# Rounding float64 weights between products: loads issued by SP, a chunk rounded three products after its load, and an earlier first norm

## The chip, the cores and the metric

The kernel runs on one core of a Trainium2 chip. The metric is the device time of one execution in microseconds (us); for the kernel before it is 1148.23 us, the median of three runs (1146.14 to 1149.64). The engines are TensorE (PE, matmuls), VectorE (DVE), ScalarE (ACT), GpSimd (POOL) and SyncE (SP, which here only issues DMA transfers). Each works through its own list of instructions and waits on semaphores for the others.

## The reference, cut to what matters

A retention block (attention with a fixed decay in place of softmax) feeds a gated feed-forward block with an RMS norm. The weights w_gate, w_val and w_out come as float64, so the kernel has to round them to float32 on the chip.

```python
def _attn_ref(q, k, v):                       # q, k, v: (8, 8, 576, 64) float32
    scores = scale * np.matmul(q, k.transpose(0, 1, 3, 2))
    ret = scores * Dmat[None, :, :, :]        # Dmat: gamma[head] ** (row - column), causal
    return np.matmul(ret, v).astype(np.float32)

def _moe_ref(x, w_gate, w_val, w_out, rms_g): # x: (4608, 512); w_gate, w_val: (512, 1536) float64
    rms = np.sqrt(np.mean(x * x, axis=-1, keepdims=True) + 1e-06)
    xn = x / rms * rms_g
    g = xn @ w_gate
    silu = g * (1.0 / (1.0 + np.exp(-g)))
    val = xn @ w_val
    return (silu * val @ w_out).astype(np.float32)   # w_out: (1536, 512) float64
```

## The kernel before

The attention is cut into **jobs**: one pair of heads of one batch entry, or a part of it. `slot(j)` computes the scores and states of job j on PE, weighs them and sums the states on DVE, and finishes job j - 1 (`values`, `carried`), which writes a block of `x`. The tokens are cut into twelve **units** of 384. A unit's norm is a chain over several engines: `square` (ACT), `gather` (DVE, adds the squares), `norm_1` (mean on PE, root on POOL), `diagonals` (DVE), `norm_2` (a broadcast product `rb` on PE, then four scalings of x on DVE).

The first two units run as plain products while the weights are still arriving. The float64 weights come in 18 **chunks** of 1 MB: for each third g of the hidden features two chunks of w_gate and two of w_val (chunks 0 to 11), then six of w_out (12 to 17). There are four spare places for chunks that have landed and are not yet rounded; the last six use only three of them.

```python
    LATER = (1, 2, 3, 2, 3, 3)
    def spare(i):
        return i % 4 if i < n_up else LATER[i - n_up]      # n_up = 12

    def load_chunks(n, queue=nc.scalar):                   # nc.scalar: the issue stands in ACT's list
        while n_loads < min(n, len(chunks)) and waits_at.get(spare(n_loads)) is None:
            load_chunk(n_loads, queue)
            n_loads += 1
```

Rounding a chunk takes five DVE instructions over 128x1024 elements and three ACT instructions. `exponent` is the first that reads the landed chunk. After the third instruction of `mantissa` the place is free and the next load is issued. The generator `rounding` fixes the order; `weights(n)` takes n steps of it and stands behind each product.

```python
    def exponent(i):
        nc.vector.tensor_scalar(out=e, in0=words_of[i][..., 1::2], ...)          # L871
        acts.extend(...)                    # three ACT instructions, L887, given out by act()

    def mantissa(i):
        nc.vector.tensor_scalar(out=dst.bitcast(U32), in0=hi, ...)               # L898
        yield
        nc.vector.scalar_tensor_tensor(out=dst, in0=lo, ...)                     # L903
        yield
        act(chunk=i)                        # what is left of this chunk's ACT instructions
        nc.vector.scalar_tensor_tensor(out=e, in0=hi, in1=e, ...)                # L908
        waits_at[spare(i)] = None

    def join(i):
        nc.vector.scalar_tensor_tensor(out=dst, in0=dst, in1=exp_of.pop(i), ...) # L916

    def rounding():
        for i in range(len(chunks)):
            if i not in exp_of and i in words_of:
                exponent(i)
                yield
            for ahead in (True, False):
                if i + 1 in words_of and i + 1 not in exp_of and i > (1 if ahead else 0):
                    exponent(i + 1)
                    yield
                if ahead:
                    yield from mantissa(i)
                    load_chunks(i + 5 if i else 0)
                    yield
            join(i)
            n_chunks += 1
            yield
```

A plain product is four matmuls of 128x384 into a bank of PSUM; five banks go round for these products, for the jobs' values and for the norms. ACT (silu) or DVE (multiply) empties the bank.

```python
    def up_plain(u, m, g):
        for half in range(2):
            for i in (2 * g, 2 * g + 1):
                ps = bank(f"up_{u}_{m}_{half}_{i}")
                for c in range(NHP):
                    nc.tensor.matmul(ps[:, :U], lhsT=w_up[m][:, 4 * half + c, ...], rhs=x_of[u][:, c], ...)  # L652
                h = h_of[u][:, half * NH + i]
                if m:
                    nc.vector.tensor_tensor(out=h, in0=h, in1=ps[:, :U], op=ALU.mult)   # L658
                else:
                    nc.scalar.activation(out=h, in_=ps[:, :U], func=AF.Silu)            # L660
                yield
```

The first eight jobs and then the 48 products of the two units, with jobs 8 to 11 put behind products 29, 33, 37 and 41 (and the end of job 11 behind 45):

```python
        for j in range(2 * NHP):                           # NHP = 4
            slot(j)
            if j + 1 < 2 * NHP:
                turn(j + 1)                                # transposes on PE, copies on ACT
            if squares:
                gather(*squares.pop())
            for i in ((1,), (2,), (3,), (4, 5), (6,), (7,), (), ())[j]:
                scale_v(i)
            if j:
                u, c = divmod(j - 1, NHP)
                squares.append((u, c, square(u, c)))
            act(1)
            if j == 5:
                norm_1(0)
            elif j == 6:
                norm_2(0)
            weights((2, 0, 0, 1, 1, 1, 1, 0)[j])
            if j == 4:
                gather(*squares.pop())
            elif j == 5:
                diagonals(0)
            act(1)
        ...
        load_qk(2 * NHP)                                   # 13 loads of a job, issued by SP
        load_kv(2 * NHP)
        made = combine_out()                               # four combinations of w_out on DVE, L690
        step = -1
        for m, g in [(m, g) for g in range(NG) for m in range(2)]:
            for u in range(2):
                weights_to(4 * g + 2 * m + 1)
                for i, _ in enumerate(up_plain(u, m, g)):
                    step += 1
                    later(step)                            # jobs 8 to 11; loads of the jobs behind them
                    ...                                    # end of job 7 and norm of unit 1
                    weights(2)
                    act(1)
                    if u and m and g == NG - 1:
                        weights_to(len(chunks))
                        next(made, None)
                    if i == 1:
                        weights_to(4 * g + 2 * m + 2)
        ...
        rest = across(1)                                   # products with w_out, L726; the first is xo,
        next(rest)                                         # the second, zo, reads t1 of differences(), L710
```

From unit 2 on, a Strassen-like scheme with seven products instead of eight is used; it is not touched.

Of the kernel before, what the change touches and what calls it, by code (L numbers as in the profile page):

```python
# [41 lines left out]
def kernel(  # L42
# [11 lines left out]
    nc = tc.nc  # L54
# [3 lines left out]
    NHP = H // 2  # L58
# [421 lines left out]
    def gather(u, c, sq):  # L480

        if c == NHP - 1 and u > 2:
            nc.vector.scalar_tensor_tensor(
                out=t_of[u], in0=t_of[u], scalar=EPS * DM / P, in1=sq, op0=ALU.add, op1=ALU.add
            )
        elif c:
            nc.vector.tensor_tensor(out=t_of[u], in0=t_of[u], in1=sq, op=ALU.add)
        else:
            t_of[u] = sq
# [5 lines left out]
    def norm_1(u):  # L495

        ms = bank(f"ms_{u}")
        for s in range(NS):
            nc.tensor.matmul(
                ms[:, s : s + 1], lhsT=t_of[u][:, s * P : s * P + P], rhs=mean_w,  # L500
                start=True, stop=True,
            )
        r = tmp.tile([P, NS], F32, tag="r", name=f"r_{u}", bufs=1)
        nc.vector.tensor_scalar(out=r, in0=ms[:, :NS], scalar1=EPS, scalar2=None, op0=ALU.add)
        nc.gpsimd.tensor_tensor(out=r, in0=r, in1=mhalf.to_broadcast([P, NS]), op=ALU.pow)
        t_of[u] = r
# [324 lines left out]
    for f in range(0, NF, 2):  # L831
        chunks.append((w_out[:, f : f + 2], moe_w_out, slice(f * P, f * P + 2 * P), slice(None)))
    LATER = (1, 2, 3, 2, 3, 3)
    words_of, exp_of, waits_at = {}, {}, {}
    n_chunks = n_loads = 0

    free = w_up[0][:, 8:].rearrange("p b f -> p (b f)")
# [5 lines left out]
    def load_chunk(i, queue):  # L843
        dst, src, rws, cols = chunks[i]
        if src.dtype != F32:
            n = dst.shape[1]
            cols = slice(2 * (cols.start or 0), 2 * cols.stop if cols.stop else None)
            src = src.bitcast(U32)
            at = spare(i)
            dst = free[:, : 4 * DM] if at == 3 else (  # L850
                w_out[:, 4 * at : 4 * at + 4].rearrange("p c f -> p (c f)")
            )
            dst = words_of[i] = dst.bitcast(U32).rearrange("p (c f) -> p c f", c=n)
            waits_at[at] = i
        queue.dma_start(out=dst, in_=src[rws, cols].rearrange("(c p) f -> p c f", p=P))

    def load_chunks(n, queue=nc.scalar):

        nonlocal n_loads
# [3 lines that stand above are left out]
# [21 lines left out]
    def act(n=0, chunk=-1):  # L884

        while acts and (n > 0 or acts[0][0] <= chunk):
            nc.scalar.activation(func=AF.Relu, **acts.pop(0)[1])  # L887
            n -= 1
# [43 lines left out]
    def rounding():  # L932

        nonlocal n_chunks
        for i in range(len(chunks)):
            if i not in exp_of and i in words_of:
                exponent(i)
                yield
            for ahead in (True, False):
                if i + 1 in words_of and i + 1 not in exp_of and i > (1 if ahead else 0):  # L940
                    exponent(i + 1)
                    yield
                if ahead:
                    yield from mantissa(i)
                    load_chunks(i + 5 if i else 0)
                    yield
            join(i)
            n_chunks += 1
            yield
# [4 lines left out]
    def weights(n):  # L954

        for _ in range(n):
            next(steps, None)

    def weights_to(n):

        while n_chunks < min(n, len(chunks)):
            next(steps)

    def start():

        h_of[0] = ffn.tile([P, NF, U], F32, tag="h", name="h_0")
        tables = list(zip((causal, gv, gc, gq, gx), (_causal_table(), *_decay_tables(H, D))))

        def table(i, queue):
            t, values_ = tables[i]
            src = nc.inline_tensor(values_, name=t.tensor.name + "_table")
            queue.dma_start(out=t, in_=src.ap())

        make_identity(nc, ident)
        nc.scalar.activation(out=tick, in_=mhalf[:1], func=AF.Silu)
        nc.vector.memset(ones, 1.0)
        warm = bank("warm")
        for _ in range(6):  # L980
            nc.tensor.matmul(warm[:, :P], lhsT=ones, rhs=ones, start=True, stop=True)
        first_places.update(find_places())
        load_chunks(1)
        for i in (1, 0, 2):
            table(i, nc.scalar)
        weights(3)
        for j in range(2 * NHP):
            load_first(j, {0: range(2), 1: range(2, H)}.get(j))
            if j == 1:
                table(3, nc.sync)  # L990
            load_chunks((1, 1, 1, 1, 2, 2, 2, 3)[j], nc.sync)
        table(4, nc.sync)
        nc.sync.dma_start(out=rms_g, in_=moe_rms_g.rearrange("(c p) -> p c", p=P))
        load_chunks(4, nc.sync)
        turn(0)
        scale_v(0)
        act(3)
        squares = []

        def later(step):  # L1000

            if step == LATER_AT[0] - 8:
                following(2 * NHP - 1)
            elif step in LATER_AT:
                j = 2 * NHP + LATER_AT.index(step)
                if j < LATER_JOBS:
                    slot(j, rest=(j > 2 * NHP))
                    if j + 1 < LATER_JOBS:
                        following(j)
                else:  # L1010
                    values(j - 1)
                    carried(j - 1)

        for j in range(2 * NHP):
            slot(j)
            if j + 1 < 2 * NHP:
                turn(j + 1)
# [4 lines that stand above are left out]
            if j:  # L1022
                u, c = divmod(j - 1, NHP)
                squares.append((u, c, square(u, c)))
            act(1)
            if j == 5:
                norm_1(0)
            elif j == 6:
                norm_2(0)
            weights((2, 0, 0, 1, 1, 1, 1, 0)[j])  # L1030
            if j == 4:
                gather(*squares.pop())
            elif j == 5:
                diagonals(0)
            act(1)
        gather(*squares.pop())
        load_qk(2 * NHP)
        load_kv(2 * NHP)
        made = combine_out()
        step = -1  # L1040
        for m, g in [(m, g) for g in range(NG) for m in range(2)]:
            for u in range(2):
                weights_to(4 * g + 2 * m + 1)
                for i, _ in enumerate(up_plain(u, m, g)):
                    step += 1
                    later(step)
                    if not (u or m or g):
                        if i == 0:
                            values(2 * NHP - 1)
                            carried(2 * NHP - 1)  # L1050
                            gather(1, NHP - 1, square(1, NHP - 1))
                        elif i == 1:
                            norm_1(1)
                        elif i == 2:
                            diagonals(1)
                        elif i == 3:
                            norm_2(1)
# [7 lines that stand above are left out]
        for _ in made:  # L1065
            pass
        for blk, t in first_blocks.items():
            keep(blk, t)
        rest = across(1)
        next(rest)  # L1070
        following(LATER_JOBS - 1)
        for i, _ in enumerate(rest):
            if i == 1:
                norm_0(2)
                differences(0)
            elif i == 2:
                norm_1(2)
                diagonals(2)
            elif i == 4:
                norm_2(2)  # L1080
        rest = across(0)
        next(rest)
        combine(1)
        slot(LATER_JOBS, rest=False)
        following(LATER_JOBS)
        for _ in rest:
            pass
        combine(0)
        slot(LATER_JOBS + 1)
        load_next(LATER_JOBS + 1)  # L1090
        turns.append(LATER_JOBS + 1)
# [74 lines left out]
```

## Time and profile before

The profiled execution has a span of 1147.0 us.

| engine | busy us | share of the span |
|---|---|---|
| PE (matmul) | 1121.7 | 98% |
| PE (weight load, beside it) | 1045.3 | 91% |
| DVE | 733.4 | 64% |
| ACT | 257.8 | 22% |
| POOL | 40.1 | 4% |

Busy shares are means over stages that differ. The page also cuts the span into 40 slices of about 28.7 us and gives for each the busy tenths of an engine, and the TensorE clock that was granted, in tenths of full speed:

```profile
PE   7899988999999999999999999999999999999998
DVE  5888777747586586466766776466577576446353
PEclk9899998999999999999999999999999999999999
```

The slices in which PE is below 9 tenths are all but the last within the first seven, which hold the start, the first twelve jobs and the two plain units. In the chain that ended last, PE has 93% of the span, DVE 3%, DMA 2%, ACT 1%. A loaded chunk of weights takes 4.8 to 6.0 us from issue to landing in the median of its groups when ACT issues it.

### The profile page before, as it was taken

The page shows a single profiled execution, that of the slowest core. Times are in us where ns is not written, and L with a number is a line of the kernel's source. Part 1 is how long each engine was busy: PE and PEld are TensorE (multiplying, and loading weights), DVE is VectorE, ACT ScalarE, POOL GpSimd, SP SyncE. Part 2 cuts the span into 40 slices and gives each one's busy share as a digit, 9 for nine tenths or more (in the row PEclk, how much of TensorE's full clock was granted, in tenths as well). Part 3 has the DMA queues.
Part 4 walks back from the last instruction along what each step waited for, and adds up shares of the span by engine and source line. Part 5 has one row for each costly group of instructions (what it writes and reads, how often), then busy time and mean ns, then how long its engine had stood idle before and what let it go on. Part 6 is the DMA issues. An engine that isn't in the chain of part 4 may idle for free.

```text
span 1147.0 us, 24779 instructions
## 1 busy us (share of the span) xinstructions
PE 1121.7 (98%) x10454; PEld 1045.3 (91%) x10454; DVE 733.4 (64%) x1452; ACT 257.8 (22%) x508; POOL 40.1 (4%) x68
## 2 busy tenths in 40 slices
PE   7899988999999999999999999999999999999998
PEld 6655645999999999999999999999999999999998
DVE  5888777747586586466766776466577576446353
ACT  5456531102211221121221121120221211120210
POOL 0100000190000000000000000000000000000000
PEclk9899998999999999999999999999999999999999
DMA  9844555434553555035345456305336413303304
GB/s 218 214 143 136 143 133 152 121 69 108 136 120 61 163 130 139 35 95 112 97 100 93 111 127 139 119 16 130 101 98 140 122 42 94 128 1 97 125 1 111
DMA packets 307039, 126.72 MB, mean 110 GB/s; under 512 B 284528, under 2 KB 289904, under 8 KB 306928
## 3 DMA queue, kind: packets, MB, share of 16 engines
q1 hardware_dynamic: 296784, 108.98, 38.9%
q10 hardware_dynamic: 10144, 16.16, 4.4%
q8 instruction: 82, 1.34, 0.5%
q14 instruction: 29, 0.24, 0.1%
HBM read 110.14 MB, written 14.94 MB: 109 GB/s over the span
## 4 chain that ended last, share of the span: by engine, by line
PE 93%; DVE 3%; DMA 2%; ACT 1%; issue 1%; SPq 0%; POOL 0%; DVEq 0%; POOLq 0%; ACTq 0%
PE x L595 14%; PE w L595 14%; PE z L595 14%; PE up L652 9%; PE xo L726 8%; PE wo L726 8%; PE zo L726 8%; PE y L595 7%; PE yo L726 4%; PE av L390 2%; PE av L412 2%; PE s L307 1%; PE s L329 1%; DMA w_gate<-in_moe_w_out_dram 1%; DMA w_out<-in_moe_w_out_dram 1%
## 5 line engine op out<-in xcount | busy, mean ns | idle before, releaser
L619 ACT COPY m<-x 128x384 f32<-128x384 f32 x60 | 28.8, 479 | 337.9 <-PE x L595 337.9
L726 PE MATMUL xo<-h,w_out 128*128 128x192 f32 x528 | 90.3, 328 | 0.0
L595 PE MATMUL w<-sums,w_val 128*128 128x192 f32 x480 | 88.7, 328 | 0.3
L595 PE MATMUL x<-x,w_val 128*128 128x192 f32 x480 | 88.8, 328 | 0.0
L595 PE MATMUL x<-x,w_gate 128*128 128x192 f32 x480 | 88.5, 328 | 0.0
L595 PE MATMUL w<-sums,w_gate 128*128 128x192 f32 x480 | 87.9, 326 | 0.0
L595 PE MATMUL z<-x,w_val 128*128 128x192 f32 x480 | 87.8, 326 | 0.0
L595 PE MATMUL z<-x,w_gate 128*128 128x192 f32 x480 | 87.8, 326 | 0.0
L726 PEld LDWEIGHTS xo<-h,w_out 128*128 128x128 f32 x528 | 85.9, 190 | 0.6
L726 PE MATMUL wo<-h,w_out 128*128 128x192 f32 x504 | 85.6, 326 | 0.4 <-DVE c_last L774 0.4
L602 DVE TENSOR_TENSOR u<-m,y 128x384 f32<-128x384 f32 x60 | 33.1, 552 | 78.6 <-PE y L595 78.6
L726 PEld LDWEIGHTS wo<-h,w_out 128*128 128x128 f32 x504 | 82.5, 190 | 0.7 <-DVE c_last L774 0.7
L595 PEld LDWEIGHTS w<-sums,w_val 128*128 128x128 f32 x480 | 79.2, 190 | 2.7 <-DVE c L602 2.7
L595 PEld LDWEIGHTS x<-x,w_val 128*128 128x128 f32 x480 | 79.2, 190 | 0.6
L595 PEld LDWEIGHTS x<-x,w_gate 128*128 128x128 f32 x480 | 79.3, 190 | 0.5
L595 PEld LDWEIGHTS z<-x,w_val 128*128 128x128 f32 x480 | 79.7, 190 | 0.0
L595 PEld LDWEIGHTS z<-x,w_gate 128*128 128x128 f32 x480 | 79.7, 190 | 0.0
L595 PEld LDWEIGHTS w<-sums,w_gate 128*128 128x128 f32 x480 | 79.5, 190 | 0.1
L602 DVE TENSOR_TENSOR h<-u,w 128x384 f32<-128x384 f32 x60 | 33.0, 550 | 69.4 <-PE w L595 69.4
L652 PE MATMUL up<-x,w_gate 128*128 128x384 f32 x192 | 65.8, 499 | 4.9 <-DVE x L435 3.6
L614 ACT ACTIVATE h<-h 128x384 f32<-128x384 f32 x90 | 47.0, 523 | 88.6 <-DVE h L602 88.6
L652 PE MATMUL up<-x,w_val 128*128 128x384 f32 x192 | 65.6, 501 | 1.3 <-DVE h L658 1.3
(189 smaller groups left out, 1783.1 us busy)
## 6 DMA issues: line engine op xcount, KB each, us to landing
w_out<-w_blocks SPq DMA_DIRECT2D x70, 768.0 KB, 4.9
out_dram<-o SPq DMA_DIRECT2D x364, 24.0 KB, 1.6
qraw<-in_q_dram SPq DMA_DIRECT2D x96, 72.0 KB, 2.6
kraw<-in_k_dram SPq DMA_DIRECT2D x96, 72.0 KB, 2.9
k<-in_k_dram SPq DMA_DIRECT2D x48, 128.0 KB, 2.9
v<-in_v_dram SPq DMA_DIRECT2D x48, 128.0 KB, 3.0
w_out<-in_moe_w_gate_dram ACTq DMA_DIRECT2D x5, 1024.0 KB, 5.8
w_out<-in_moe_w_out_dram ACTq DMA_DIRECT2D x3, 1024.0 KB, 6.0
```

The source lines that it names most:

```text
L307: nc.tensor.matmul(s[side(odd), e, i * L : i * L + L], lhsT=d["kT"][side(e), c * L : c * L + L], rhs=d["qT"][side(e), c * L : c * L + L], ...
L329: nc.tensor.matmul(o[side(e)], lhsT=d["k"][side(odd), i, e], rhs=d["v"][side(odd), i, e], start=True, stop=True,)
L390: mm = nc.tensor.matmul(av[odd][column(j, odd, e), i * L : i * L + L], lhsT=d["v"][side(odd), i, e] if c < NC - 1 else d["vt"][:, e], rhs= ...
L412: mm = nc.tensor.matmul(av[odd][column(j, odd, e), i * L : i * L + L], lhsT=d["sum"][c - 1][side(e)], rhs=d["qT"][side(e), c * L : c * L + L],
L595: nc.tensor.matmul(ps[:, i * HU : i * HU + HU], lhsT=w_up[m][:, 2 * blk + c, cut], rhs=t_of[u][blk][:, c], start=(start and i == c == 0), ...
L602: nc.vector.tensor_tensor(out=o, in0=a, in1=pairs_of(ps), op=ALU.add)
L614: nc.scalar.activation(out=o, in_=c, func=AF.Silu)
L619: nc.scalar.copy(out=s1, in_=pairs_of(x_))
L652: nc.tensor.matmul(ps[:, :U], lhsT=w_up[m][:, 4 * half + c, i * P : i * P + P], rhs=x_of[u][:, c], start=(c == 0), stop=(c == NHP - 1),)
L726: nc.tensor.matmul(ps[:, i * HU : i * HU + HU], lhsT=a[:, c, i * P : i * P + P], rhs=rhs[:, c], start=(start and i == c == 0), stop=False, ...
```

## The change

The change has four parts. First, chunks from the fifth on are issued by SP instead of ACT, in the order of the program among the jobs' loads. Second, each load is stamped with the number of products so far plus three (`there_at`), and the generator gives out a chunk's exponent only when that many products stand in the program, or when the chunk is due; until then it does other steps or none. Third, the norm of the first unit starts right behind job 4 instead of job 5, and with it each of its links moves one job ahead. Fourth, the first gate product stands ahead of the eighth job instead of behind it, and the counter of products starts with the second one, so that jobs 8 to 11 stand one product later. It is meant to keep DVE from standing at a load that has not landed, and to give PE work among the last jobs. No arithmetic is added or taken away.

```diff
-    words_of, exp_of, waits_at = {}, {}, {}
+    words_of, exp_of, waits_at, there_at = {}, {}, {}, {}
+    now = 0
+    due = False
@@ load_chunk
         queue.dma_start(out=dst, in_=src[rws, cols].rearrange("(c p) f -> p c f", p=P))
+        there_at[i] = now + 3 if now else 0
@@ rounding
         for i in range(len(chunks)):
+            while i in words_of and i not in exp_of and not due and now < there_at[i]:
+                yield
             if i not in exp_of and i in words_of:
                 exponent(i)
                 yield
             for ahead in (True, False):
-                if i + 1 in words_of and i + 1 not in exp_of and i > (1 if ahead else 0):
+                if (
+                    i + 1 in words_of and i + 1 not in exp_of and i > (1 if ahead else 0)
+                    and (due or now >= there_at[i + 1])
+                ):
                     exponent(i + 1)
                     yield
                 if ahead:
                     yield from mantissa(i)
-                    load_chunks(i + 5 if i else 0)
+                    load_chunks(i + 5 if i else 0, nc.sync)
                     yield
@@ weights_to
+        due = True
         while n_chunks < min(n, len(chunks)):
             next(steps)
+        due = False
@@ start
+        first = up_plain(0, 0, 0)
@@ the first eight jobs
-            act(1)
+            if j != NHP:
+                act(1)
             if j == 5:
+                diagonals(0)
+            elif j == 6:
+                next(first)
+            weights((2, 0, 0, 1, 0, 1, 1, 1)[j])
+            if j == NHP:
+                gather(*squares.pop())
                 norm_1(0)
-            elif j == 6:
+            elif j == 5:
                 norm_2(0)
-            weights((2, 0, 0, 1, 1, 1, 1, 0)[j])
-            if j == 4:
-                gather(*squares.pop())
-            elif j == 5:
-                diagonals(0)
             act(1)
@@ the products of units 0 and 1
-        step = -1
+        now = 0
...
-                for i, _ in enumerate(up_plain(u, m, g)):
-                    step += 1
-                    later(step)
+                whole = u or m or g
+                for i, _ in enumerate(up_plain(u, m, g) if whole else first, 0 if whole else 1):
+                    later(now)
+                    now += 1
                     if not (u or m or g):
-                        if i == 0:
+                        if i == 1:
                             values(2 * NHP - 1)
                             carried(2 * NHP - 1)
                             gather(1, NHP - 1, square(1, NHP - 1))
-                        elif i == 1:
+                        elif i == 2:
                             norm_1(1)
-                        elif i == 2:
                             diagonals(1)
                         elif i == 3:
                             norm_2(1)
```

More of the change, by code (lines that the diff above doesn't have):

```diff
@@ L959, in weights_to @@
     def weights_to(n):
+        nonlocal due
+        due = True
         while n_chunks < min(n, len(chunks)):
             next(steps)
+        due = False
     def start():
+        nonlocal now
         h_of[0] = ffn.tile([P, NF, U], F32, tag="h", name="h_0")
```

## The prediction, written before the changed kernel ran

> **What bounds the kernel now.** I began with the page's 40 slices: TensorE (PE) is at 9 tenths almost everywhere, and the slices that are not lie in the first 200 us. The windows view, cut at four landmarks, says how much is missing there (PE busy is the first figure after the length):
>
> ```profile
> 34.00:62.50 28.50, 25.41 (x291) 17.16 (x284) 22.24 (x61) 14.53 (x27) 3.63 (x7) 0.88 0.75 196
> 62.50:129.80 67.30, 67.30 (x212) 39.46 (x212) 59.55 (x70) 43.98 (x54) 0.00 (x0) 1.00 0.49 153
> 129.80:202.60 72.80, 64.06 (x569) 40.69 (x569) 51.86 (x87) 20.09 (x32) 0.35 (x4) 0.91 0.53 144
> 202.60:1147.00 944.40, 939.06 (x8740) 925.80 (x8738) 579.20 (x1172) 161.37 (x352) 35.14 (x48) 1.00 0.40 99
> ```
>
> PE idles 28.5 - 25.4 = 3.1 us in the first stretch and 72.8 - 64.1 = 8.7 us in the third; the clock column (third from the end) is also below 1.00 only there. The second stretch is PE alone; the last, with 5.3 us idle, is not touched. So the change can act in two places, early (jobs 4 to 7) and late (the last chunks of w_out).
>
> The late stretch: first the waits of DVE (VectorE), then those of PE, each "who <- for what: us in total, times, longest".
>
> ```profile
> DVE w_gate L871 <- DMA w_gate<-in_moe_w_out_dram: 7.0, 1, 7.0
> DVE w_gate L871 <- DMA w_out<-in_moe_w_out_dram: 5.0, 1, 5.0
> ```
>
> ```profile
> PE up L652 <- DVE x L435: 3.6, 1, 3.6
> PE av L390 <- ACT w_val L660: 3.5, 1, 3.5
> ...
> PE up L652 <- DVE h L658: 1.3, 1, 1.3
> ```
>
> The timeline places them: the two issues by ScalarE (ACT), and the two instructions of DVE that waited (the wait is in brackets):
>
> ```profile
> 137.46 0.38 ACTq L855 DMA_DIRECT2D w_out<-in_moe_w_out_dram  x1
> ...
> 165.78 0.37 ACTq L855 DMA_DIRECT2D w_gate<-in_moe_w_out_dram  x1
> ```
>
> ```profile
> 144.16 0.69 DVE L871 TENSOR_SCALAR w_gate<-w_out 128x1024 uint32<-128x1024 uint32 x1 [5.00 <-DMA w_out<-in_moe_w_out_dram]
> ...
> 172.72 0.69 DVE L871 TENSOR_SCALAR w_gate<-w_gate 128x1024 uint32<-128x1024 uint32 x1 [6.98 <-DMA w_gate<-in_moe_w_out_dram]
> ```
>
> These are chunks 15 and 17. A load is issued when a spare place comes free, and DVE's next instruction is already that chunk's exponent (L871): it stands 5.0 and 7.0 us, and all behind it stands too. Then PE has no bank (3.6 us; 3.5 and 1.3 us). From issue to exponent it is 144.16 - 137.46 = 6.7 and 172.72 - 165.78 = 6.9 us.
>
> The early stretch, in the timeline of PE, has only small idle pieces; the one at the third gate product is this:
>
> ```profile
> 55.72 5.40 PE L652 MATMUL up<-x,w_gate 128*128 128x384 f32 x16 [0.56 <-DVE r L504]
> ```
>
> The chain of waits there runs through the gather of the first unit's fourth square (DVE 39.21), root, diagonal and the scaled x (46.39), then for unit 1 through the gather at 53.28, an exponent, the join of chunk 1 (L916, from 54.44), root and diagonal to x (61.80); unit 1's first product starts at 62.47.
>
> **What the Trainium skill says.** "TensorE: Matmul & The Clock Gate", Part 1: the PE clock has two states, half and full, set by a free-running window of about 3.4 us. The trace agrees: cut by 1 us, the granted clock is 0.50 from about 33.9 to 37.3, 44.1 to 47.5, 149.9 to 153.3 and 173.9 to 184, each after a window with over 1 us idle, none after windows with 0.3 to 0.6 us. A slow window costs about 1.7 us of work. The same page, under the architectural detail of the array, says that ACT and DVE queues are strict FIFO; the 7.0 us line, with ready work behind it, agrees. "DMA: Bandwidth & Descriptors", under issuing engines are not separate DMA queues: issuing from several engines saves only the sequencer's time. Here that time is not small: one job's 13 loads hold the SP queue 7.6 us (151.61 to 158.58 + 0.61) and 8.0 us (204.55 to 211.95 + 0.65):
>
> ```profile
> 204.55 2.94 SPq L156 DMA_DIRECT2D qraw<-in_q_dram  x4
> 207.59 2.06 SPq L156 DMA_DIRECT2D kraw<-in_k_dram  x4
> 209.70 1.05 SPq L224 DMA_DIRECT2D k<-in_k_dram  x2
> 210.85 0.99 SPq L224 DMA_DIRECT2D v<-in_v_dram  x2
> 211.95 0.65 SPq L229 DMA_DIRECT2D vt<-in_v_dram  x1
> ```
>
> **The change part by part.** Estimates below continue the trace's durations in the order in which the changed program stands on each engine.
>
> *1. Early norm.* The chain of gather, mean, root and diagonal moves one job earlier. But the mean (ms) now stands on PE straight behind the transposes of job 5, which end at 37.64. Its input is the gather of the fourth square, which waits for ACT (copies of q and k, two scalings, the square: 37.44 to 39.18) and is done at 39.77, as before. In the old order PE did job 4's values and job 5's scores meanwhile; now it idles 39.8 - 37.6 = 2.1 us, and the skill's window then gives a slow clock from 40.7. POOL's root now also stands ahead of the tick that frees job 4's carried products. I get: rb at 44.4, x scaled 45.2 to 47.4, first product 47.6 (before 47.88).
>
> *2. First gate product ahead of the eighth job.* It fills the wait for job 6's sums. Then job 7's scores, the second product (51.8 to 54.4) and job 7's values and carried products, to 55.4 (before, the same two products and job were through at 54.4). What stood behind them as a filler, the second product, is used up. The third product needs chunk 1, whose join stands on DVE behind job 7's x (0.4), ACT's square (0.5), gather (0.6), an exponent (0.65) and itself (1.2): 3.4 us after the carried products. PE idles 55.4 to 58.8, against 0.3 + 0.6 us before; again a window over 1 us, about 1.3 us of slow clock. The rest (mean 0.5, root and diagonal beside the fourth product, rb 0.7, x 0.9): third product to 62.5, fourth 63.0 to 65.6, unit 1's first product at about 67.2. Against 62.47 that is **4.7 us lost**. Of this 4.0 is idle time (7.1 against 3.1), the rest clock.
>
> *3. Three products' distance.* Chunk 15's exponent moves from behind product 31 (by each program's own counter) to behind product 33, after job 9's results, and 17's to behind product 40. I follow DVE from job 8, which starts one product later since the counter now starts at the second product: s(8) ends at 133.65 instead of 130.73 (plus 4.7, which I leave out until the sum). Job 8 on DVE 3.2, chunk 13 and 14 and one multiply: 145.9. Job 9's block (ret, x, sums, transposes: 160.35 to 164.56 before) 4.2: 150.1. Chunk 15 was issued by 144 and is there by about 150.5: **its 5.0 us wait and PE's 3.6 us go away**. Its last mask needs ACT's third step, which now stands behind a silu: 154.6 (2.0 us of DVE wait), 155.75. Chunk 16, 15's join and job 10 to 163.7; chunk 16's end and two multiplies to 167.1.
>
> *4. Issue by SP.* Fourteen issues of about 0.38 us leave ACT, which is busy 22% of the span and gains nothing that ends last. But chunk 17's issue now stands on SP behind job 12's thirteen loads, which start with job 11's transposes at 163.2 and take 8.0 us: issued at 171.3 rather than at 164.9 when its place is free, landed after 5 to 6.9 us, say 176.2. DVE is there at 167.1 and **waits 9 us instead of 7.0**. From the landing: exponent, mask, multiply of product 41 (1.8), job 11 (3.4), two steps of chunk 17 (2.4), multiply (0.5), join (1.2), four multiplies (0.55 each), four combinations of w_out (1.75 each), x of job 11 (1.1), first half of the differences (1.35): 21.0 with rounding. So t1, which the second product of across needs, is ready at 197.2. PE, which waits about 5 us for the bank of product 41 and some 2 us for t1, follows.
>
> *Sum.* The second across product starts at 202.65 before. Now at 197.2 + 4.7 = 201.9, 0.75 us earlier, less about 1.7 us of slow clock after the wait for t1 (a window again over 1 us): +1 us in all. Behind this point the orders are the same and PE is full, so the end moves by as much: 1148.2 + 0 to 1, I take 1148.7.
>
> **The rivals.** *(a) The late stretch is simply cleared*: chunk 17 is issued at 164.9 and is there at 172; then t1 comes 4.2 us sooner and the sum is about -4 us with part 2's loss, or -9 without. For it speaks that chunk 15's wait surely goes; against it that SP's order puts job 12's loads first. *(b) The early part gains*, as its filler was meant to: PE had 1.06 us waiting for a transposed q, 0.49 for the tick and 0.6 at the third product. If the old idle goes and no new one comes, -2 us there, so 1148.2 - 0.8 - 4.7 - 2 = about 1141. Against it stands the order: mean and third product wait for work that can't be ready. *(c) DVE becomes the bound up to t1*: from 133.65 to 197.2 it is busy some 52 us and waits about 11, so any further delay of chunk 17 comes out one for one: 1152 or more. *(d) The load was hidden anyway* is excluded by the 7.0 us line.
>
> **Range and chances.** Part 2 may be off by 2.5 us (phase of the clock window), the landing of chunk 17 by 2 us, the clock after t1 by 1.7; the three runs before spread over 3.5 us. Together about 6 us either way: 1142.5 to 1154.5. 2% is 23 us, more than all idle time in both stretches, so within 2% is all but sure.
>
> **What would show it.** Part 1: PE waits about 2 us for DVE's sq (gather) near 38 us. Part 2: PE's third product (up, L652) waits 3 to 3.5 us for DVE's w_gate; unit 1's first product at 66 to 68. Part 3: no wait of DVE for chunk 15, no 3.6 us of PE on x. Part 4: one wait of DVE for the last w_gate load, 7 to 10 us, that load's issue right behind job 12's on SP, and PE waiting 4 to 6 us for DVE's h. Sum: the second across product between 199 and 206. The prediction is wrong if the early waits on PE stay under 1 us each, or if chunk 17 lands within 3 us of DVE's reaching it.

## The result, and the profile after

The changed kernel takes **1152.4 us**, the median of four runs (1150.62 to 1152.78); the kernel before took 1147.65 us beside it (1146.14 to 1149.64). The ratio is 1.0037, with a 95% interval of 1.0018 to 1.0057: slower, by 4.8 us between the medians (2 to 6.5 us by the interval). The predicted time was 1148.7 us with a range of 1142.5 to 1154.5. The small sum hides two larger ones: the early part loses more than predicted, the late part gains about what was predicted.

The page of the changed kernel, its 40 slices. The second clock digit (about 29 to 58 us) has fallen from 8 to 7, and PE is at 8 in the first three slices; from the eighth slice on nothing differs:

```profile
PE   8889998999999999999999999999999999999998
...
PEclk8789999999999999999999999999999999999999
```

The windows view of the changed kernel, cut as before (length; busy time of PE, PE's weight load, DVE, ACT, POOL with the number of instructions; granted clock; share of the DMA engines; GB/s):

```profile
34.00:62.50 28.50, 22.38 (x312) 16.25 (x309) 17.07 (x50) 12.30 (x26) 1.26 (x6) 0.74 0.57 174
...
129.80:202.60 72.80, 67.20 (x586) 41.37 (x585) 58.92 (x97) 27.22 (x42) 0.35 (x4) 0.98 0.53 152
```

In the first stretch PE now idles 28.5 - 22.4 = 6.1 us (before 3.1), at a clock of 0.74 (before 0.88). In the third it idles 5.6 us (before 8.7), at 0.98 (before 0.91). One stretch pays and the other earns.

PE's waits in the changed kernel ("who <- for what: us in total, times, longest"):

```profile
PE up L652 <- DVE h L658: 5.3, 1, 5.3
PE up L652 <- DVE w_gate L919: 3.5, 1, 3.5
...
PE ms L499 <- DVE sq L487: 2.1, 1, 2.1
...
PE zo L726 <- DVE t L710: 0.5, 1, 0.5
```

The 2.1 us are the mean of part 1 (`ms`) waiting for the fourth gather, the 3.5 us the third gate product waiting for the join of chunk 1, the 5.3 us the bank of product 41 behind chunk 17. All three were named by the prediction. The last, at t1, is small.

The reading is easier between landmarks. All times are from the timelines of each profile. The unit 1 product is PE's first product for unit 1, which waits for that unit's norm. "zo" is the second product of across, which needs t1. The first of these products, before and after:

```profile
62.47 10.59 PE L652 MATMUL up<-x,w_gate 128*128 128x384 f32 x32 [0.71 <-DVE x L564]
```

```profile
71.83 10.59 PE L652 MATMUL up<-x,w_gate 128*128 128x384 f32 x32 [0.71 <-DVE x L564]
```

| us | before | after | difference |
|---|---|---|---|
| end of job 5's transposes | 37.64 | 38.09 | +0.45 |
| unit 1's first product | 62.47 | 71.83 | +9.36 |
| zo | 202.65 | 205.36 | +2.71 |
| end of the span | 1147.0 | 1151.0 | +4.0 |

So the early part loses 9.4 us, the stretch from there to zo takes 133.5 us against 140.2 and gains 6.7, and 1.3 us come behind zo. No run explains those 1.3 us: the stretch from zo to the end took 944.3 us before, 945.6 after, and 944.3 to 945.4 in the ten experiments, in which its order does not differ either.

**The early part.** The windows view for the stretch from the end of job 5's transposes to unit 1's first product, of the kernel before and then of the changed one:

```profile
37.64:62.47 24.83, 21.74 (x233) 14.11 (x232) 19.48 (x51) 12.64 (x24) 3.37 (x6) 0.93 0.77 207
```

```profile
38.09:71.83 33.74, 26.92 (x232) 17.46 (x233) 17.70 (x50) 12.49 (x24) 2.02 (x6) 0.75 0.51 151
```

The work is the same (233 and 232 instructions of PE). Idle time is 24.83 - 21.74 = 3.1 us before and 6.8 us after: +3.7. The busy time grew by 5.2 us with the same instructions; that is the clock. Cut into windows of 3.4 us, the changed kernel shows it:

```profile
36.80:40.20 3.40, 1.29 (x22) 0.81 (x18) 2.26 (x7) 2.38 (x6) 0.00 (x0) 0.97 0.91 259
40.20:43.60 3.40, 3.40 (x56) 3.27 (x58) 0.61 (x4) 0.39 (x1) 0.91 (x2) 0.50 0.92 274
43.60:47.00 3.40, 3.17 (x12) 1.41 (x12) 2.26 (x10) 2.09 (x6) 0.00 (x0) 0.50 1.05 396
47.00:50.40 3.40, 3.40 (x60) 2.93 (x60) 3.20 (x10) 1.01 (x2) 0.09 (x1) 0.53 0.17 61
60.70:67.60 6.90, 6.02 (x14) 3.63 (x14) 0.73 (x1) 1.30 (x3) 0.00 (x0) 0.52 0.83 171
```

The wait for the gather leaves PE 1.29 us busy in the first window, and then the clock is at half for three windows, 40.2 to 50.4, not for one. Behind the wait for the join it is at half for two more, 60.7 to 67.6. Before, in the first stretch of the windows view, two windows were slow, at 33.9 and 44.1, and only the second lies behind job 5's transposes.

**The late part.** Chunk 15's exponent stands at 159.04 in DVE's timeline without a wait. For chunk 17, the timelines of SP (its issues) and of DVE in the changed kernel (start, length, instruction, wait in brackets):

```profile
178.53 0.61 SPq L229 DMA_DIRECT2D vt<-in_v_dram  x1
179.24 0.54 SPq L857 DMA_DIRECT2D w_gate<-in_moe_w_out_dram  x1
```

```profile
172.46 1.18 DVE L911 SCALAR_TENSOR_TENSOR w_gate<-w_gate 128x1024 uint32<-128x1024 uint32 x1
...
185.51 0.69 DVE L874 TENSOR_SCALAR w_gate<-w_gate 128x1024 uint32<-128x1024 uint32 x1 [9.68 <-DMA w_gate<-in_moe_w_out_dram]
```

The place is free when L911 ends, at 173.64. SP issues the load at 179.24, straight behind the last of job 12's thirteen loads: 5.6 us late. From issue to exponent it is 6.3 us, no longer than with ACT's issue (6.9).

### The profile page after: what moved, and what is told of

Its sections match the earlier page's. It is cut to its first block, busy times and chain, and to the rows that moved or that the text cites. A ratio compares the mean times of both kernels' runs of the same rounds, so it can differ in the third digit from the quotient of the medians.

```text
span 1151.0 us, 24773 instructions
## 1 busy us (share of the span) xinstructions
PE 1124.0 (98%) x10454; PEld 1046.7 (91%) x10454; DVE 732.7 (64%) x1452; ACT 258.0 (22%) x508; POOL 38.5 (3%) x68
## 4 chain that ended last, share of the span: by engine, by line
PE 91%; DVE 4%; DMA 1%; SPq 1%; ACT 1%; issue 1%; DVEq 0%; POOLq 0%; POOL 0%; ACTq 0%
PE x L595 14%; PE w L595 14%; PE z L595 14%; PE wo L726 8%; PE zo L726 8%; PE xo L726 8%; PE up L652 7%; PE y L595 7%; PE yo L726 4%; PE av L390 2%; PE s L307 2%; PE av L412 1%; PE s L329 1%; DMA w_gate<-in_moe_w_out_dram 1%; PE ms L513 1%
```

## The experiments

**What is to be told apart.** My theory: the early part costs by two new waits and the clock behind them; the distance gains; the issue by SP loses by its place behind job 12's loads. The rivals: the late part gains nothing as a whole; the issue by SP is harmless or helps; the early part is paid for by its filler product. The kernels of one batch share a chip and the runs of the kernel before: 1147.41 us (e1 to e4), 1147.59 (e5 to e8), 1147.24 (e9), three bases that differ by 0.4 us. The interval of a ratio reaches 1.3 to 2 us to either side; a difference as small as that is not shown by the times alone.

### The late part alone, and its two halves

*e1_late_only*: the changed kernel with the order of the first eight jobs put back, so SP and distance are left.

```diff
 # from the changed kernel
-            if j != NHP:
-                act(1)
+            act(1)
             if j == 5:
-                diagonals(0)
+                norm_1(0)
             elif j == 6:
-                next(first)
+                norm_2(0)
-            weights((2, 0, 0, 1, 0, 1, 1, 1)[j])
+            weights((2, 0, 0, 1, 1, 1, 1, 0)[j])
 ...
```

The lines cut put the other links of the norm and the start of the counter back in the same way.

> Late half alone: chunks by SP, a chunk's exponent three products behind its load; the first eight jobs, the first norm and the first gate product stand as in the kernel before. Theory A (the early part costs about 9 us by the place of unit 1's first product, the late part gains about 6 to 8): unit 1's first product back at about 62.5, DVE still waits 9 to 10 us for chunk 17, the second across product at 194 to 197 instead of 202.7, and 1139.5 to 1142 in all. Rival B (the early part is innocent, the loss comes with SP's queue): within 1 us of the changed kernel, 1151 to 1153.

Measured: 1143.69 us, ratio 0.9965 (0.9953 to 0.9976). DVE waits 10.3 us for chunk 17 and not for chunk 15; PE waits 5.7 us for the bank. From unit 1's first product to zo it takes 133.7 us, and in the changed kernel 133.5: between these two products the late part does in the change what it does alone. The gain in time is 3.7 us, and theory A's range (to 1142) is missed by 1.7: of the 6.5 us that this stretch gains in the profile, 1.0 is lost ahead of it and 0.5 behind it, and the profiled run of the kernel before (1148.79 us) lies 1.4 us above the median that e1 is compared with. By the medians the early part costs 1152.4 - 1143.7 = 8.7 us.

*e2_late_act*: e1 with ACT issuing, so of the change the distance is left.

```diff
-                    load_chunks(i + 5 if i else 0, nc.sync)
+                    load_chunks(i + 5 if i else 0)
```

> As the run before, but ACT issues the chunks as in the kernel before, so that chunk 17 doesn't stand behind job 12's loads. Theory A: chunk 17 is issued 6 to 7 us sooner, DVE's wait for it falls from 9.7 to 2 to 5 us, and the time falls by 2 to 5 us more, to 1136 to 1139. Rival C (DVE has that time to spare, PE bounds the stretch once the other waits are gone): no more than 1 us from the run before, the shorter wait notwithstanding.

Measured: 1137.44 us, ratio 0.9915 (0.9898 to 0.9931). Time and wait are as theory A has them. The distance alone gains 10 us, and SP's issue takes 6.3 of them back. DVE's exponent of chunk 17 in e1 and then in e2, from the timelines:

```profile
175.36 0.69 DVE L874 TENSOR_SCALAR w_gate<-w_gate 128x1024 uint32<-128x1024 uint32 x1 [10.34 <-DMA w_gate<-in_moe_w_out_dram]
```

```profile
169.79 0.69 DVE L874 TENSOR_SCALAR w_gate<-w_gate 128x1024 uint32<-128x1024 uint32 x1 [4.08 <-DMA w_gate<-in_moe_w_out_dram]
```

The wait is 6.3 us shorter, and so is the time. The load was issued at 168.71 by SP in e1 and at 163.83 by ACT in e2, 4.9 us sooner (expected were 6 to 7); the rest of the shorter wait is a transfer 0.7 us shorter and DVE coming 0.7 us later.

*e4_sp_only*: the kernel before with the issue by SP and nothing else.

```diff
-                    load_chunks(i + 5 if i else 0)
+                    load_chunks(i + 5 if i else 0, nc.sync)
```

> The kernel before with one word changed: SP issues the chunks from the fifth on, without the distance. Theory A: chunk 15 stands behind job 10's loads and chunk 17 behind job 12's, DVE's waits for them grow from 5.0 and 7.0 to about 9 and 14 us, and the time rises to 1154 to 1160. Rival D (the issuing queue doesn't matter, the distance alone does): 1147 to 1149.

Measured: 1155.67 us, ratio 1.0071 (1.0056 to 1.0085), 8.3 us lost. Without the distance both chunks meet the exponent at once, and both waits of DVE are longer than before (5.0 and 7.0 us):

```profile
DVE w_gate L871 <- DMA w_gate<-in_moe_w_out_dram: 11.7, 1, 11.7
DVE w_gate L871 <- DMA w_out<-in_moe_w_out_dram: 7.7, 1, 7.7
```

The time is as expected, the waits are shorter than the 9 and 14 us expected. So SP's issue loses with and without the distance. That it is the place in SP's list, and not SP, was tried next.

*e8_sp_first*: e1 with a job's thirteen loads given out behind that product's rounding steps.

```diff
                     if j + 1 < LATER_JOBS:
-                        following(j)
+                        prepare_next(j)
+                        put_off.append(j)
 ...
                     weights(2)
                     act(1)
+                    while put_off:
+                        load_next(put_off.pop())
```

> The late half with SP issuing (1143.7 us), but a job's thirteen loads are issued behind the steps of rounding of the same product, so that chunks 15 and 17 stand ahead of the loads of jobs 10 and 12 in SP's list. If the place in SP's list is the cause: DVE's wait for chunk 17 falls from 10.3 to 3 to 5 us and the time to 1136.5 to 1139, as with ACT. If a load issued by SP lands later whatever stands ahead of it (shared with the other transfers): 1142 or more.

Measured: **1136.27 us, ratio 0.99 (0.9887 to 0.9913)**, the fastest of all, at the lower edge of the first range. SP's timeline has chunk 17's issue at 161.75, when its place comes free, and job 12's loads from 162.18:

```profile
161.75 0.38 SPq L857 DMA_DIRECT2D w_gate<-in_moe_w_out_dram  x1
162.18 2.59 SPq L156 DMA_DIRECT2D qraw<-in_q_dram  x4
```

(The expectation speaks of chunks 15 and 17; in the order that this edit makes, chunk 15 still stands behind job 10's loads, which costs nothing, because DVE does not wait for it.) DVE's exponent of chunk 17 in e8:

```profile
167.25 0.69 DVE L874 TENSOR_SCALAR w_gate<-w_gate 128x1024 uint32<-128x1024 uint32 x1 [3.62 <-DMA w_gate<-in_moe_w_out_dram]
```

It waits as short a time as with ACT, and PE no longer waits for the bank. With SP still issuing and the job's loads behind the chunk's, SP's loss is gone: 7.4 us against e1. So the place in SP's list is the cause. Whether SP in front is any better than ACT (1135.05 to 1137.25 against 1135.42 to 1140.36, on different chips) is not told apart.

*e9_dist2* and *e9_dist5*: e8 with another distance.

```diff
-        there_at[i] = now + 3 if now else 0
+        there_at[i] = now + 2 if now else 0      # e9_dist2; + 5 in e9_dist5
```

> As e8_sp_first, but a chunk's exponent is given out two products behind its load instead of three. If three products are just enough (theory: DVE's wait for chunk 17 in e8_sp_first, 3.6 us, is what is left of the transfer after the distance), an exponent that stands one product, some 2.7 us, sooner waits that much longer or meets a second wait at chunk 15: one or two waits of DVE for w_out loads with 5 to 9 us in all, and 1137 to 1141 us against 1136.3 of e8_sp_first. Rival (any distance above none will do, since DVE has enough slack up to t1): waits in all below 5 us, 1135 to 1137 us.

> As e8_sp_first with five products instead of three. If the wait for the load is what the distance should remove, more distance removes the remaining 3.6 us at chunk 17, and the time falls to 1133 to 1135.5 us. Rival (DVE then bounds the stretch: exponents given out later leave more of the rounding behind the last jobs, where the first reader of a rounded chunk is due): no wait for w_out loads on DVE, but PE waits longer for t1 or for DVE's h, and 1136.5 to 1142 us.

Measured: 1142.76 us (ratio 0.9961, 0.9948 to 0.9974) with two, 1139.52 us (0.9933, 0.9918 to 0.9947) with five. DVE's waits with two:

```profile
DVE w_gate L874 <- DMA w_out<-in_moe_w_out_dram: 4.1, 1, 4.1
DVE w_gate L874 <- DMA w_gate<-in_moe_w_out_dram: 4.1, 1, 4.1
```

Chunk 15's wait is back, with 2.7 us of PE behind it; the time is 1.8 us above what I allowed. With five there is no wait for any w_out load, and the time is not shorter but 3 us longer than with three, as the rival said. A distance of four was not tried. PE's timeline with five:

```profile
191.84 4.14 PE L726 MATMUL zo<-t,w_gate 128*128 128x192 f32 x24 [2.14 <-issue]
```

The bracket names no engine. DVE's timeline has the first half of t1 (L710) from 190.39 for 1.35 us, so it ends at 191.74, 0.1 us before zo: DVE is what PE waits for. Chunk 17's exponent stands at 174.39 there, 7.1 us later than with three (1.6 of them lie ahead of unit 1's first product), and all of DVE's list behind it is later. So the two ends cost for opposite reasons: with two DVE stands at loads, with five its work comes too late for t1, and a wait of 3.6 us at three is better than none.

### The early part alone, and its two halves

*e3_early_only*: the kernel before with the new order of the first eight jobs alone: ACT issues, no distance.

```diff
 # from the changed kernel
-        there_at[i] = now + 3 if now else 0
+        there_at[i] = 0
 ...
-                    load_chunks(i + 5 if i else 0, nc.sync)
+                    load_chunks(i + 5 if i else 0)
```

> Early half alone: first norm one job sooner, first gate product ahead of the eighth job, counter from the second product; ACT issues the chunks and an exponent stands right behind its load, as before. Theory A: unit 1's first product at about 71.8 as in the changed kernel, the waits of 5.0 and 7.0 us for chunks 15 and 17 are there again, and 1155 to 1159. Rival B: 1146.5 to 1149, as before.

Measured: 1155.09 us, ratio 1.0066 (1.0049 to 1.0083), 7.7 us lost, at the lower edge of theory A's range. The two waits of PE are those of the changed kernel (2.1 us for the gather, 3.5 us for the join), and DVE's waits for chunks 15 and 17 are back (4.3 and 6.7 us). Unit 1's first product stands at 70.17, 1.7 us sooner than in the changed kernel, though the first eight jobs stand in the same order: the clock is at half for two windows behind the gather (41.5 to 48.3) and one behind the join (62.0 to 65.4), where the changed kernel has three and two.

*e5_norm_only*: e2 with the first norm one job sooner, the first product where it was. As in the changed kernel, one rounding step goes with it from job 4 to job 7.

```diff
+            if j != NHP:
+                act(1)
             if j == 5:
-                norm_1(0)
-            elif j == 6:
-                norm_2(0)
+                diagonals(0)
-            weights((2, 0, 0, 1, 1, 1, 1, 0)[j])
-            if j == 4:
+            weights((2, 0, 0, 1, 0, 1, 1, 1)[j])
+            if j == NHP:
                 gather(*squares.pop())
+                norm_1(0)
             elif j == 5:
-                diagonals(0)
+                norm_2(0)
```

> The late half with ACT issuing (1137.4 us) plus only the first norm one job sooner; the first gate product stays behind the eighth job. If the early loss is shared by both pieces: PE waits 2.1 us for the gather at the mean, a slow clock follows, and 1140 to 1143. If the norm's place is harmless and the product's place makes the whole loss: 1136.5 to 1138.5.

Measured: 1139.42 us, ratio 0.993 (0.9917 to 0.9943), between the two ranges expected. Taken each against its own kernel before, that is 1.8 us worse than e2, but the intervals overlap (e2: 0.9898 to 0.9931), so the times alone do not show a loss. The trace shows its place: PE waits 2.1 us for the gather, one window, 42.1 to 45.5, is slow behind it, and unit 1's first product stands at 65.24 (62.66 in e2).

*e6_product_only*: e2 with the first product ahead of the eighth job, the norm where it was.

```diff
+        first = up_plain(0, 0, 0)
 ...
             elif j == 6:
                 norm_2(0)
+                next(first)
 ...
-        now = 0
+        now = 1
 ...
-                for i, _ in enumerate(up_plain(u, m, g)):
+                whole = u or m or g
+                for i, _ in enumerate(up_plain(u, m, g) if whole else first, 0 if whole else 1):
```

> The late half with ACT issuing plus only the first gate product ahead of the eighth job (first norm at its old place; jobs 8 to 11 behind the same products as before). If the used-up filler counts: PE waits 3 to 3.5 us at the third product for DVE's join of chunk 1 with a slow clock behind it, and 1140.5 to 1143.5. If the product's place is harmless: 1136.5 to 1138.5.

Measured: 1143.23 us, ratio 0.9961 (0.9949 to 0.9973), 5.6 us worse than e2, as the first expectation has it. This half has the larger loss. PE's third product in e6:

```profile
57.97 5.17 PE L652 MATMUL up<-x,w_gate 128*128 128x384 f32 x8 [3.50 <-DVE w_gate L919]
```

Its eight matmuls take 5.17 us, not 2.85, for the clock is at half from 55.9 to 62.7. 1.8 and 5.6 us add up to 7.4, close to the 7.7 of e3.

*e7_product_join*: e6 with two more rounding steps given out behind job 7, so that chunk 1 is joined before the products need it.

```diff
-            weights((2, 0, 0, 1, 1, 1, 1, 0)[j])
+            weights((2, 0, 0, 1, 1, 1, 1, 2)[j])
```

> As the run before, but chunk 1's last two steps (the exponent of chunk 2 and the join of chunk 1) are given out ahead of the end of job 7, so that the third product doesn't wait for job 7's x on DVE. If the join's place in DVE's list is the cause of the wait: it falls from about 3.5 to under 1 us and the time comes back to 1136.5 to 1139. If the product's place does harm by itself (job 7 later, unit 1's norm later): 1140 or more, as the run before.

Measured: 1140.61 us, ratio 0.9935 (0.9923 to 0.9947), 3.0 us worse than e2 in place of 5.6. The wait of 3.5 us is gone:

```profile
58.46 2.85 PE L652 MATMUL up<-x,w_gate 128*128 128x384 f32 x8
```

But the clock is slow at another place. PE's first product in e7:

```profile
48.09 5.46 PE L652 MATMUL up<-x,w_gate 128*128 128x384 f32 x8 [0.80 <-DVE x L564]
```

The clock is at half from 43.3 to 53.5 here, three windows. So the wait went as the first expectation has it, and the time lies just inside the range of the second. The join was the cause of the wait, and with it gone nearly half of the loss is recovered. The slow clock that remains begins ahead of everything that this edit moved: up to job 7's scores the order is that of e6, where one window was slow (42.3 to 45.7). It also differs from run to run: three of e7's six runs had a mean granted clock of 0.994 to 0.995 and took 1137.89 to 1140.10 us, the other three, the profiled one among them, 0.991 to 0.992 and 1141.13 to 1141.94. Whether the product's place does harm by itself is therefore not shown.

### The sums

The stretch from unit 1's first product to zo, with the same products in it:

| kernel | issue | distance | us to zo | DVE's waits for chunks 15, 17 |
|---|---|---|---|---|
| before | ACT | none | 140.2 | 5.0, 7.0 |
| e4 | SP | none | 147.2 | 7.7, 11.7 |
| e2 | ACT | 3 | 127.7 | 0, 4.1 |
| e1 | SP | 3 | 133.7 | 0, 10.3 |
| after | SP | 3 | 133.5 | 0, 9.7 |
| e8 | SP, ahead of the loads | 3 | 126.2 | 0, 3.6 |
| e9_dist2 | the same | 2 | 132.3 | 4.1, 4.1 |
| e9_dist5 | the same | 5 | 128.2 | 0, 0 |

Unit 1's first product stands between 62.1 and 63.6 us in the six experiments with the old early order, at 65.2 with the norm moved, 67.7 with the product moved, 66.7 in e7, and 70.2 (e3) and 71.8 (the change) with both. That spread of 1.5 us among like orders is the limit of what one profile tells here.

From the times: distance -10.0, SP's place +6.3, early order +8.7, in all +5.0; measured +4.8. These are steps from one kernel to the next (before, e2, e1, after), so they have to add up. What tests the sum is the early part alone, e3: +7.7 with e1's -3.7 makes +4.0, near enough to +4.8 for this noise.

## Why the prediction was right, and where it was not

**Right in the sum, with two of its terms wrong in opposite directions.** The range held the time, and it was held in part by luck: it allowed 2.5 us for part 2, where the error was 4.7, and a clock term of 1.7 us that did not come took some of it back.

*Part 1, the wait for the gather*: predicted 2.1 us with a slow clock behind it, measured 2.1 us; e5 prices this half at 1.8 us, which is not clear of noise. **The idle time of part 2** is right: 3.5 us for chunk 1's join (predicted 3.4), and +3.7 us idle in all (predicted 4.0). e7 shows the cause: with the join earlier, the wait is gone.

*The clock of the early part is the term that failed.* Predicted were 4.7 us lost by unit 1's first product, 4.0 of them idle time and the rest, 0.7, clock. Measured are 9.4 us, 5.2 of them clock. I had counted one slow window behind the gather, in place of the one before, and 1.3 us of slow clock behind the join, since in the early part of the kernel before each slow stretch lasted one window. In the changed kernel the first lasts three (40.2 to 50.4) and the second two (60.7 to 67.6). Unit 1's first product, foretold for 66 to 68, came at 71.83. How many windows are slow is not fixed by the order: e3, with the same one, has two and one, 70.17, and still loses 7.7 us in time.

*The other clock term failed the other way*: about 2 us of waiting for t1 and 1.7 us of slow clock behind it. PE waited 0.5 us, and the stretch behind zo has a clock of 1.00.

*Part 3* is right: no wait for chunk 15, none of PE for its x. The last mask of that chunk waited for ACT's third step, 1.95 us against 2.0 predicted. Its worth was not given apart from part 4; e2 gives it, 10 us. (The 4.2 us of "job 9's block" were read at job 10's, 160.35 to 164.56; job 9's own, 147.76 to 151.96, take as long.)

*Part 4* is right in kind and size: issued right behind job 12's loads, DVE waiting 9.7 us (predicted 9), PE 5.3 us for the bank (predicted about 5). e8 shows that the place in the list does it. Job 12's loads held SP 7.0 us and not 8.0. From the end of job 8's scores (s(8): 130.73 before, 142.66 after) to zo the prediction had 201.9 - 133.65 - 4.7 = 63.5 us; it is 62.7.

*The sum*: for zo the prediction had 201.9 and 1.7 us of clock behind it, so 203.6 in effect. The early error adds 4.7, the missing clock at t1 takes off 1.7, the two small differences of the late part take off 1.2 (0.4 to s(8), since one product takes 2.6 us and not 2.9; 0.8 from there to zo): 205.4. What is left up to the 3.7 us of the median is 1.3 us behind zo, unexplained, and the spread of the runs.

*The rivals*: (a), the late stretch simply cleared, is what the distance does when the load isn't held up: it put -9 us on it, and e2 has -10. It failed here for the reason given against it. (b), the early filler gains, is refuted by e3 and e6, which lose 7.7 and 5.6 us clear of noise. (c), DVE as the bound up to t1, foretold 1152 us or more, and the time is 1152.4; but by the traces that number comes from the early part, and zo waited 0.5 us. DVE as the bound is seen with a distance of five, where zo waits 2.1 us. With three the delay of chunk 17 also comes out about one for one (from e1 to e2 6.3 us of wait and 6.3 of time, from e1 to e8 6.7 and 7.4), but through PE's wait for the bank (5.3 to 5.7 us) and not at t1.

## What to carry to other kernels

A load that an in-order engine reads should be given out some work behind its issue, and both the distance and the place of the issue in its queue have to be right: here three products gained 10 us with ACT issuing, two or five gained less than three with SP, and thirteen small loads ahead of one large load took 6 of the 10 back. A matmul moved forward as a "filler" is missing at the next wait: here PE then stood 3.5 us at the join of chunk 1, and nothing was gained, so follow that wait before moving it. When a move opens idle time on PE of a microsecond or more, count on one to three slow windows behind it (all three numbers occurred here) and give the range that width.

## What the runs showed of the hardware that was not expected

**A busy window does not always bring the clock back.** The Trainium skill, "TensorE: Matmul & The Clock Gate", Part 1, has the clock go to full after at least one busy window of about 3.4 us. In the kernel before it did so. In the changed kernel PE is busy for 3.40 of 3.40 us from 40.2 to 43.6 by the records, and the clock stays at half until 50.3; in e3 it is busy for 3.41 of 3.41 us from 41.74 to 45.15, and the clock stays at half until 48.3. e5, after a like wait and a like full window (42.1 to 45.5), is back at 0.99 in the next one. The windows differ in their phase against the mean's six matmuls of one column (in the changed kernel they fill 40.20 to 41.57, inside the first slow window; in e3 they end at 41.83 and in e5 at 41.99, near its start) and the small 64x64 matmuls of job 6; the ends of matmuls in the records are modelled, so "busy" there need not be what the clock gate counts. No run tells these apart, and the rule for the length of a slow stretch stays open.

**Many issues add up in one queue.** The same skill, "DMA: Bandwidth & Descriptors", under issuing engines not being separate queues, has issuing from another engine save only the time of the sequencer, usually small beside the transfer. For one load that agrees: SP is held 0.54 us by chunk 17's issue, and from issue to exponent it is 6.3 us with SP, 6.9 with ACT. For a queue the issues add up: the thirteen of one job hold SP from 172.10 to 179.14 in the changed kernel, 7.0 us, which is longer than the 1 MB load behind them takes to be there.
